# One SyncE queue in a fixed store/load order, in place of loads on SyncE and stores on GpSimd, in a decode-step backward kernel

## The chip, the cores and the metric

The kernel runs on one NeuronCore of a Trainium2 chip. The metric is the device time of one execution in microseconds (us). A time here is the median of the fast runs of one kernel. A ratio of two kernels is the mean time of one kernel's fast runs over that of the other's of the same rounds, so it is not quite the ratio of the medians quoted beside it.

Engines are named as in the profile: PE (TensorE), DVE (VectorE), ACT (ScalarE), POOL (GpSimd), SP (SyncE). Beside them the core has 16 DMA engines, which move all data. "Queue" is here a line of the page's queue part (q1 holds what SP issues, q0 what POOL issues, q10 what ACT issues), and "ring" is another word for it, where the order of the transfers waiting in it is meant.

## The reference

One decode step of attention with a key/value cache, plus a SwiGLU MLP, on a single token of width 640, forward and backward (the vector-Jacobian product), in bf16:

```python
xn = layernorm(x)
# A: 32 heads of 128, 8192 cached positions each
q = (xn @ wq)                       # wq 640 x 4096
p = softmax(q @ K^T / sqrt(128))    # K, V: 32 x 8192 x 128
attn = (p @ V) @ wo                 # wo 4096 x 640
# B: F = 1728
out = x + attn + (silu(xn @ w1) * (xn @ w3)) @ w2
# returned: out and the gradients of x, K, V, wq, wo, w1, w3, w2
```

The gradients of K and V are as large as K and V: 64 tiles of 2 MB are read and 64 written. The weights add 17 MB each way. About 303 MB cross the DMA engines in each execution.

## The kernel before

Ten SBUF slots of 2 MB hold K/V tiles. A tile is loaded, used, overwritten in place with its gradient, and stored. Its slot then takes the next load. Loads are issued on SyncE (`nc.sync`), stores on GpSimd (`nc.gpsimd`).

```python
def load_group(g):                    # weights of four heads, 2 x 640 KB
    wq_g = wpool.tile([P, NC, GW], BF16, name="wq_g", tag="wq_g")
    nc.sync.dma_start(wq_g[:], wq_v[:, :, g * GW:(g + 1) * GW])   # rows of 1024 B
    wo_g = wpool.tile([P, GH, D], BF16, name="wo_g", tag="wo_g")
    nc.sync.dma_start(wo_g[:], wo_v[:, g * GH:(g + 1) * GH, :])   # rows of 1280 B
    grp[g] = dict(wq=wq_g, wo=wo_g)

def load_next():
    if not pending:
        return
    kind, h = pending.pop(0)
    if kind == "K" and h % GH == GH - 1 and h // GH + 1 < NG:
        load_group(h // GH + 1)
    t = free_slots.pop(0)
    nc.sync.dma_start(t[:], (kc if kind == "K" else vc)[h])       # 128 rows of 16 KB
    kv_tiles[(kind, h)] = t

def store(kind, h):
    t = kv_tiles.pop((kind, h))
    nc.gpsimd.dma_start((dkc if kind == "K" else dvc)[h], t[:])
    free_slots.append(t)
    load_next()
# ... (cut: transposes, dots, softmax, outer products)
def finish_group(g):
    # ... (cut)
    nc.gpsimd.dma_start(dwo_v[:, g * GH:(g + 1) * GH, :], wo_g[:])
    # ... (cut)
    nc.gpsimd.dma_start(dwq_v[:, :, g * GW:(g + 1) * GW], wq_g[:])
# ... (cut: the MLP, which stores the gradients of w1, w2, w3 on GpSimd)
for h in range(H):
    # ... (cut)
    sums(h); outer_v(h, 0, J // 2); outer_v(h, J // 2, J)
    store("V", h)
    # ... (cut: MLP after head 1; K of head h+1; outer_k)
    store("K", h)
    # ... (cut)
```

## Time and profile before

| | before |
|---|---|
| time, us (3 runs) | 749.74 (749.73 to 751.52) |
| span of the profiled run, us | 748.2 |
| bytes moved, mean rate | 304.62 MB, 407 GB/s |

The profile's page of the kernel before: busy time of each engine, then the span in 40 equal slices (busy tenths of the DMA engines, and GB/s), then DMA queues with packets, MB and share of the 16 engines' time.

```profile
span 748.2 us, 25141 instructions
## 1 busy us (share of the span) xinstructions
PE 594.4 (79%) x11263; PEld 550.9 (74%) x11263; DVE 445.3 (60%) x771; ACT 329.8 (44%) x668; POOL 53.6 (7%) x93
...
DMA  8999999999999999999999999999998999999976
GB/s 324 387 420 423 421 422 429 427 414 430 423 420 425 424 428 422 425 429 427 390 362 411 424 428 422 379 424 430 427 417 316 423 426 430 425 427 426 425 294 259
...
q1 hardware_dynamic: 21828, 151.35, 48.9%
q0 software_dynamic: 12960, 151.34, 48.2%
q8 instruction: 88, 1.44, 0.7%
```

No compute engine is near its limit, and the DMA engines are busy almost everywhere. q1 holds the loads (SyncE), q0 the stores (GpSimd), and q8 the instruction fetches, 88 packets of 16 KB. The slices show short holes in the middle and at the end. The table of 10 us windows has them larger (columns: window and its length, busy time and count of each engine, TensorE clock, DMA share, GB/s):

```profile
core 0: us, PE busy (x) PEld busy (x) DVE busy (x) ACT busy (x) POOL busy (x), PEclk, DMA share, GB/s
380.00:390.00 10.00, 8.28 (x215) 7.92 (x214) 7.94 (x15) 3.07 (x7) 0.00 (x0) 1.00 0.80 313
560.00:570.00 10.00, 8.43 (x168) 8.08 (x169) 9.07 (x13) 5.03 (x10) 1.07 (x2) 1.00 0.73 280
720.00:730.00 10.00, 4.48 (x130) 4.29 (x131) 8.52 (x7) 0.16 (x1) 0.53 (x1) 1.00 0.46 192
```

The page's list of DMA issues (count, KB each, median us from issue to landing) shows loads waiting long behind stores, the small-row weight loads longest:

```profile
out_dram<-kv POOLq DMA_DIRECT2D x64, 2048.0 KB, 19.7
kv<-in_A_k_cache_dram SPq DMA_DIRECT2D x32, 2048.0 KB, 47.1
...
wq_g<-in_A_wq_dram SPq DMA_DIRECT2D x8, 640.0 KB, 68.0
wo_g<-in_A_wo_dram SPq DMA_DIRECT2D x8, 640.0 KB, 62.8
```

And in the list of waits PE stands still for K loads (total us, times, longest):

```profile
PE pT L260 <- DMA kv<-in_A_k_cache_dram: 70.7, 7, 24.5
```

The page's group of the K/V transposes says the same (shapes, count, busy us and mean ns; then PE's idle time before them and what ended it):

```profile
L260 PE MATMUL pT<-ident_f,kv 128*128 128x128 f32 x2048 | 334.7, 287 | 75.3 <-DMA kv<-in_A_k_cache_dram 70.7
```

### The profile page before, as it was taken

What the parts mean: (1) busy time and instruction counts of PE and PEld (TensorE: products, weight loads), DVE (VectorE), ACT (ScalarE), POOL (GpSimd) and SP (SyncE); (2) the same over time, 40 slices, a digit from 0 to 9 for tenths busy, and PEclk for the clock granted to TensorE, in tenths of its full rate; (3) what the DMA queues carried; (4) which work ended last, traced back from release to release, by engine and by line L of the source; (5) the groups of instructions that cost most, each with busy time, mean ns of one, the idle gap of its engine ahead of it and who ended that gap; (6) DMA issues with size and microseconds to landing.
All of it is one profiled execution on the core that took longest, in us unless ns stands there. A gap on an engine that the chain in (4) does not pass through costs nothing. (4 is left out here: it accounts for less than half of the span.)

```text
span 748.2 us, 25141 instructions
## 1 busy us (share of the span) xinstructions
PE 594.4 (79%) x11263; PEld 550.9 (74%) x11263; DVE 445.3 (60%) x771; ACT 329.8 (44%) x668; POOL 53.6 (7%) x93
## 2 busy tenths in 40 slices
PE   2988798993889999429986999829989499998961
PEld 2886688883778888329886888829888488887860
DVE  4368857671577657506676456653576565756664
ACT  2541254553345555215554555505555255554530
POOL 0001100100001000100001000010000100010001
PEclk9995999997799999859999899968999799999995
DMA  8999999999999999999999999999998999999976
GB/s 324 387 420 423 421 422 429 427 414 430 423 420 425 424 428 422 425 429 427 390 362 411 424 428 422 379 424 430 427 417 316 423 426 430 425 427 426 425 294 259
DMA packets 35183, 304.62 MB, mean 407 GB/s; under 512 B 2836, under 2 KB 14036, under 8 KB 18692
## 3 DMA queue, kind: packets, MB, share of 16 engines
q1 hardware_dynamic: 21828, 151.35, 48.9%
q0 software_dynamic: 12960, 151.34, 48.2%
q8 instruction: 88, 1.44, 0.7%
q10 hardware_dynamic: 288, 0.33, 0.2%
q14 instruction: 19, 0.16, 0.0%
HBM read 151.67 MB, written 151.34 MB: 405 GB/s over the span
## 5 line engine op out<-in xcount | busy, mean ns | idle before, releaser
L260 PE MATMUL pT<-ident_f,kv 128*128 128x128 f32 x2048 | 334.7, 287 | 75.3 <-DMA kv<-in_A_k_cache_dram 70.7
L262 ACT COPY KT<-pT 128x512 f32<-128x512 f32 x512 | 293.8, 588 | 227.1 <-PE pT L260 186.4
L260 PEld LDWEIGHTS pT<-ident_f,kv 128*128 128x128 f32 x2048 | 229.6, 146 | 78.3 <-issue 76.0
L271 PEld LDWEIGHTS <-KT 128*128 128x128 bf16 x4096 | 179.2, 99 | 28.4 <-ACT KT L262 19.2
L321 DVE TENSOR_TENSOR kv<-qd,U 128x4096 bf16<-128x4096 bf16 x64 | 144.3, 2285 | 48.5 <-PE hb L345 48.5
L321 DVE TENSOR_TENSOR kv<-qd,P 128x4096 bf16<-128x4096 bf16 x64 | 145.7, 2286 | 42.1 <-PE hb L340 42.1
L271 PE MATMUL sA<-cz,KT 128*128 128x64 bf16 x2048 | 100.6, 194 | 5.8 <-issue 2.4
L271 PE MATMUL dA<-cz,KT 128*128 128x64 bf16 x2048 | 98.7, 193 | 6.4 <-ACT KT L262 6.3
L345 PEld LDWEIGHTS <-kv 128*128 128x128 bf16 x2048 | 68.6, 98 | 13.2 <-issue 13.0
L345 PE MATMUL hb<-U,kv 128*128 128x64 bf16 x2048 | 69.5, 193 | 9.3 <-DVE U L342 6.4
L358 POOL DMA_DIRECT2D out_dram<-kv x64 | 34.9, 546 | 567.8 <-DVE kv L321 309.1
L340 PE MATMUL hb<-P,kv 128*128 128x64 bf16 x2048 | 69.3, 193 | 0.3 <-issue 0.3
L340 PEld LDWEIGHTS <-kv 128*128 128x128 bf16 x2048 | 68.8, 99 | 0.4 <-issue 0.4
L336 DVE SCALAR_TENSOR_TENSOR U<-dA,P 128x64 bf16<-128x64 f32 x32 | 7.4, 231 | 77.0 <-PE dA L271 77.0
L347 ACT COPY od_g<-hb 128x2 f32<-128x2 f32 x32 | 5.1, 161 | 79.0 <-PE hb L345 45.6
L285 ACT CAST qd<-pT 128x256 bf16<-128x256 f32 x32 | 12.0, 375 | 54.4 <-PE pT L282 54.4
L229 DVE SCALAR_TENSOR_TENSOR KT<-wo_g,g_bc 128x640 bf16<-128x640 bf16 x32 | 26.4, 824 | 15.9 <-PE dA L271 15.4
L308 DVE RECIPROCAL rZ<-sA 128x1 f32<-128x1 f32 x32 | 5.4, 169 | 47.1 <-PE sA L301 47.1
L293 DVE TENSOR_REDUCE mrow<-sA 128x1 f32<-128x64 f32 x32 | 6.5, 203 | 33.3 <-PE sA L271 33.2
L384 DVE SCALAR_TENSOR_TENSOR wq_g<-wq_g,KT 128x512 bf16<-128x512 bf16 x40 | 26.2, 686 | 0.0
L297 DVE TENSOR_REDUCE negM<-sA 128x1 f32<-128x128 f32 x32 | 9.3, 291 | 14.5 <-PE sA L294 14.5
L301 PEld LDWEIGHTS sA<-rsum,pm_one 128*128 128x128 f32 x64 | 9.5, 187 | 11.2 <-ACT E L300 11.2
(127 smaller groups left out, 311.2 us busy)
## 6 DMA issues: line engine op xcount, KB each, us to landing
out_dram<-kv POOLq DMA_DIRECT2D x64, 2048.0 KB, 19.7
kv<-in_A_k_cache_dram SPq DMA_DIRECT2D x32, 2048.0 KB, 47.1
kv<-in_A_v_cache_dram SPq DMA_DIRECT2D x32, 2048.0 KB, 40.9
wq_g<-in_A_wq_dram SPq DMA_DIRECT2D x8, 640.0 KB, 68.0
wo_g<-in_A_wo_dram SPq DMA_DIRECT2D x8, 640.0 KB, 62.8
out_dram<-wo_g POOLq DMA_DIRECT2D x8, 640.0 KB, 16.1
out_dram<-wq_g POOLq DMA_DIRECT2D x8, 640.0 KB, 18.4
kv<-in_B_w_dram SPq DMA_DIRECT2D x2, 1728.0 KB, 18.5
```

The source lines that it names most:

```text
L229: nc.vector.scalar_tensor_tensor(junk, wo_g[:, hh, :], 1.0, g_bc[:], ALU.mult, ALU.mult, accum_out=do_c[:, hh:hh + 1])
L260: nc.tensor.transpose(pT[:, k * P:(k + 1) * P], W3[:, 4 * c + k, :], ident_f[:])
L262: nc.scalar.copy(KT[:].rearrange("p k w -> p (k w)"), pT[:])
L271: nc.tensor.matmul(out_[:, 0:J], lhsT=KTb[:, k, par, :], rhs=cz[:, par, a, J - 2 - 2 * i:ZW - 2 * i], start=(i == 0 and par == 0), stop=(p ...
L285: nc.scalar.copy(qd[:].rearrange("p a d -> p (a d)"), ps_r[:, 0:2 * DH])
L297: nc.vector.tensor_reduce(negM[:], sA[:, J:J + P], AX.X, ALU.max, negate=True)
L301: nc.tensor.matmul(sA[:, J + P:J + P + 1], lhsT=ones_b, rhs=rsum[:], start=False, stop=True, skip_group_check=True)
L321: nc.vector.tensor_tensor(dst[:, lo * DH:hi * DH].rearrange("p (j a b) -> p j a b", a=DH // 2, b=2), vec.rearrange("p (a b) -> p a b", b=2 ...
L340: nc.tensor.matmul(hb[:, 0:RW], lhsT=V3[:, j, :], rhs=P2[:, j, 0:1].to_broadcast([P, RW]), start=False, stop=(j == J - 1), skip_group_chec ...
L345: nc.tensor.matmul(hb[:, RW:2 * RW], lhsT=K3[:, j, :], rhs=U2[:, j, 0:1].to_broadcast([P, RW]), start=False, stop=(j == J - 1), skip_group ...
L358: nc.gpsimd.dma_start((dkc if kind == "K" else dvc)[h], t[:])
L384: nc.vector.scalar_tensor_tensor(wq_g[:, ci, :], wq_g[:, ci, :], 1.0, dqb, ALU.mult, ALU.mult, accum_out=dxa[:, ci, g:g + 1])
```

## The change

Intent: with one queue in program order, a weight load no longer competes with the stores' larger packets, and loads and stores take turns, one 2 MB tile each. `lag` keeps one more slot back, so that a load goes into the slot whose store was issued one store earlier, and the wait for that store leaves transfers behind it in the ring. The two small final outputs move to ScalarE's queue.

```diff
+    def fifo(out_, in_):
+        tc.keep_in_program_order(nc.sync.dma_start(out_, in_))
 ...
+    lag = [1]                      # set to 2 after the first loads
     def load_next():
-        if not pending:
+        if not pending or len(free_slots) < lag[0]:
             return
 ...
-        nc.sync.dma_start(t[:], (kc if kind == "K" else vc)[h])
+        fifo(t[:], (kc if kind == "K" else vc)[h])
 ...
     def store(kind, h):
-        nc.gpsimd.dma_start((dkc if kind == "K" else dvc)[h], t[:])
+        fifo((dkc if kind == "K" else dvc)[h], t[:])
 ...                               # likewise every weight load (nc.sync -> fifo)
 ...                               # and every weight-gradient store (nc.gpsimd -> fifo)
-    nc.sync.dma_start(out_0 ..., fin_bf[0:NC, :])
+    nc.scalar.dma_start(out_0 ..., fin_bf[0:NC, :])        # out_1 likewise
```

More of the change, by code (lines that the diff above doesn't have):

```diff
@@ L101, in load_group @@
         wq_g = wpool.tile([P, NC, GW], BF16, name="wq_g", tag="wq_g")
-        nc.sync.dma_start(wq_g[:], wq_v[:, :, g * GW:(g + 1) * GW])
+        fifo(wq_g[:], wq_v[:, :, g * GW:(g + 1) * GW])
         wo_g = wpool.tile([P, GH, D], BF16, name="wo_g", tag="wo_g")
-        nc.sync.dma_start(wo_g[:], wo_v[:, g * GH:(g + 1) * GH, :])
+        fifo(wo_g[:], wo_v[:, g * GH:(g + 1) * GH, :])
         grp[g] = dict(wq=wq_g, wo=wo_g)
@@ L138 @@
         nc.vector.memset(w2b[RB:P, NFULL - NBA, :], 0.0)
-        nc.sync.dma_start(w2b[0:RB, NFULL - NBA, :], B_w2[NFULL * P:F, :])
-    nc.sync.dma_start(w2a, B_w2[0:NBA * P, :].rearrange("(fb p) c -> p fb c", p=P))
-    nc.sync.dma_start(w2b[:, 0:NFULL - NBA, :],
+        fifo(w2b[0:RB, NFULL - NBA, :], B_w2[NFULL * P:F, :])
+    fifo(w2a, B_w2[0:NBA * P, :].rearrange("(fb p) c -> p fb c", p=P))
+    fifo(w2b[:, 0:NFULL - NBA, :],
                       B_w2[NBA * P:NFULL * P, :].rearrange("(fb p) c -> p fb c", p=P))
-    nc.sync.dma_start(w1a, w1_v[:, 0:NA, :])
-    nc.sync.dma_start(w1b, w1_v[:, NA, :])
-    nc.sync.dma_start(w3a, w3_v[:, 0:NA, :])
-    nc.sync.dma_start(w3b, w3_v[:, NA, :])
+    fifo(w1a, w1_v[:, 0:NA, :])
+    fifo(w1b, w1_v[:, NA, :])
+    fifo(w3a, w3_v[:, 0:NA, :])
+    fifo(w3b, w3_v[:, NA, :])
     for _ in range(2):
         load_next()
+    lag[0] = 2
     ident_f = consts.tile([P, P], F32, name="ident_f")
@@ L381, in finish_group @@
             nc.vector.tensor_scalar(wo_g[:, hh, :], g_bc[:], od[:, hh, 0:1], None, ALU.mult)
-        nc.gpsimd.dma_start(dwo_v[:, g * GH:(g + 1) * GH, :], wo_g[:])
+        fifo(dwo_v[:, g * GH:(g + 1) * GH, :], wo_g[:])
         for ci in range(NC):
@@ L386, in finish_group @@
             nc.vector.tensor_scalar(wq_g[:, ci, :], dqb, xn_col[:, ci:ci + 1], None, ALU.mult)
-        nc.gpsimd.dma_start(dwq_v[:, :, g * GW:(g + 1) * GW], wq_g[:])
+        fifo(dwq_v[:, :, g * GW:(g + 1) * GW], wq_g[:])
     def wrow(wi, ci):
@@ L456, in mlp @@
             nc.vector.tensor_scalar(w2a[:, b, :], g_bc[:], hcol[:, b:b + 1], None, ALU.mult)
-        nc.gpsimd.dma_start(out_8[0:NBA * P, :].rearrange("(fb p) c -> p fb c", p=P), w2a)
+        fifo(out_8[0:NBA * P, :].rearrange("(fb p) c -> p fb c", p=P), w2a)
         for b in range(NBA, NB):
             nc.vector.tensor_scalar(w2b[:, b - NBA, :], g_bc[:], hcol[:, b:b + 1], None, ALU.mult)
-        nc.gpsimd.dma_start(out_8[NBA * P:NFULL * P, :].rearrange("(fb p) c -> p fb c", p=P),
+        fifo(out_8[NBA * P:NFULL * P, :].rearrange("(fb p) c -> p fb c", p=P),
                             w2b[:, 0:NFULL - NBA, :])
         if RB:
-            nc.gpsimd.dma_start(out_8[NFULL * P:F, :], w2b[0:RB, NFULL - NBA, :])
+            fifo(out_8[NFULL * P:F, :], w2b[0:RB, NFULL - NBA, :])
         free_slots.append(mD)
@@ L490, in mlp @@
                 nc.vector.tensor_scalar(wa[:, ci, :], bc_sb[:, wi, :], xn_col[:, ci:ci + 1], None, ALU.mult)
-            nc.gpsimd.dma_start(dv[:, 0:NA, :], wa)
+            fifo(dv[:, 0:NA, :], wa)
             free_slots.append((mA, mB)[wi])
@@ L501, in mlp @@
             nc.vector.tensor_scalar(wb, bc_sb[:, wi, :], xn_col[:, NA:NC], None, ALU.mult)
-            nc.gpsimd.dma_start(dv[:, NA, :], wb)
+            fifo(dv[:, NA, :], wb)
         free_slots.append(mC)
@@ L557 @@
     nc.vector.tensor_copy(fin_bf[:], ps_o[0:2 * NC, 0:P])
-    nc.sync.dma_start(out_0.rearrange("a b (c p) -> (a b c) p", p=P), fin_bf[0:NC, :])
-    nc.sync.dma_start(out_1.rearrange("a b (c p) -> (a b c) p", p=P), fin_bf[NC:2 * NC, :])
+    nc.scalar.dma_start(out_0.rearrange("a b (c p) -> (a b c) p", p=P), fin_bf[0:NC, :])
+    nc.scalar.dma_start(out_1.rearrange("a b (c p) -> (a b c) p", p=P), fin_bf[NC:2 * NC, :])
 _INS = ['A_x', 'A_k_cache', 'A_v_cache', 'A_wq', 'A_wo', 'B_x', 'B_w1', 'B_w3', 'B_w2', 'grad_out']
```

## The prediction

> **What bounds the kernel now.** The DMA engines. The page's queue part shows 304.62 MB in a span of 748.2 us, the load and store queues holding 48.9% and 48.2% of it; the slices show 420 to 430 GB/s in most places. PE is 79% busy, DVE 60%, ACT 44%.
>
> The visible losses are small: in a table of 10 us windows 370-400 moves 366, 313 and 387 GB/s, 470-490 387 and 374, 560-580 280 and 353, 720-730 192. Against 425 GB/s these are 15 to 18 us of the mean engine. That looks like the prize, 2%.
>
> But the trace's packet records say more. From the first transfer to the last there is no instant without a data packet in flight, 743.9 us. In the deepest holes one of 16 engines is still working (7.1 us in total), and at the end one finishes 4 us after the others. Of each load's 16 completions the last comes up to 20 us after the fifteenth. One engine is always behind, hence always busy. It seems to be the one that also fetches instructions: 88 packets of 16 KB, spread evenly. Around one such fetch the interval between kv packets grew from 611 to 725 ns; I estimate 0.25 us a fetch, 22 us in all. A mean engine works about 724 us; 724 + 22 is about the 744 seen. So the straggler is the bound, and the holes are the others waiting for it.
>
> **What the change removes, adds, moves.** It removes the software queue and the competition between rings. Now 1 KB weight packets alternate with 16 KB store packets: weight loads land after 63 to 68 us (median), kv stores after 20; PE starves up to 25 us for a K load. The Trainium skill, "DMA: Bandwidth & Descriptors", section "Queues, rings and completion order", describes this round robin by packet; the trace agrees. These waits should go. By the same page, section "Issuing engines are not separate DMA queues", both queues use the same 16 engines, so no bandwidth is added; here a 16 KB packet takes 611 ns in either queue.
>
> Added: weight-gradient stores probably split like weight loads: 1024 B in 46 ns, 1280 B in 55, 3456 B in 138, instead of 4096 B in 160, 5120 in 198, 6912 in 262. Estimate over 12,224 pieces: 4.5 us per engine. A load waits for the store two places ahead, so two transfers (10 us) stay queued: no hole. The last 10 kv stores follow all loads, 50 us of queued work that hides the last compute.
>
> **On the critical path.** Only the straggler's own work: 744, plus up to 4.5, minus a few us of two-ring overhead. Holes filled on the other 15 engines buy nothing.
>
> **Prediction: 748 us, 8 in 10 between 738 and 757.** Faster by over 2%: 0.10; within 2%: 0.84; slower: 0.06.
>
> **What would show it.** Right: one hardware queue, half loads and half stores; no long K-load waits that leave the DMA idle; weight loads landing sooner; holes gone, mean rate still 403 to 412 GB/s; the last of 16 completions still late. Wrong: 425 GB/s throughout and a span near 725 us, meaning the straggler was no bound.
>
> **What would make it wrong.** Slower small HBM writes from the hardware queue (12,224 pieces at 30 ns more are 23 us); SyncE held by a DVE wait in the MLP stage with loads behind it; or a straggler cost that comes from the software queue and vanishes (about 730).

## More of the kernel before

`sums(h)`, used in some experiments, is two loops of 64 matmuls, each with its own weight load.

All runs here were taken in several sessions, on more than one chip; the kernel before took 749.8 to 750.5 us (medians) in each, so a difference of under 1 us between runs of different sessions says little.

## The result

The changed kernel takes 758.75 us (758.61 to 759.70, 4 runs), the kernel before 750.01 us in the same rounds: ratio 1.0115, 95% interval 1.0098 to 1.0133. It is slower by 1.15%, inside the 2% band that the prediction favoured, but 1.75 us above the range.

The same parts of the page, of the changed kernel:

```profile
span 756.8 us, 25031 instructions
## 1 busy us (share of the span) xinstructions
PE 601.0 (79%) x11263; PEld 561.1 (74%) x11263; DVE 447.1 (59%) x771; ACT 330.7 (44%) x668; POOL 0.7 (0%) x6
...
DMA  8999999999999999999999999999999999999996
GB/s 332 389 420 413 401 418 410 416 427 403 426 424 388 416 396 428 421 426 381 403 427 368 400 404 401 429 420 413 359 429 409 360 416 383 427 425 420 391 418 263
...
q1 hardware_dynamic: 43616, 302.69, 98.3%
q8 instruction: 88, 1.44, 0.7%
```

One queue now carries everything. The deep holes are gone, but many slices are at 359 to 405 GB/s although the DMA share is at 9 tenths: the engines are busy and move less.

Its DMA issues:

```profile
out_dram<-kv SPq DMA_DIRECT2D x64, 2048.0 KB, 21.2
kv<-in_A_k_cache_dram SPq DMA_DIRECT2D x32, 2048.0 KB, 15.7
...
wq_g<-in_A_wq_dram SPq DMA_DIRECT2D x8, 640.0 KB, 21.0
wo_g<-in_A_wo_dram SPq DMA_DIRECT2D x8, 640.0 KB, 22.6
```

The weight loads land after 21 to 23 us instead of 63 to 68, and in the page's groups PE's idle time before the K/V transposes fell from 75.3 us to 0.1:

```profile
L267 PE MATMUL pT<-ident_f,kv 128*128 128x128 f32 x2048 | 317.5, 287 | 0.1
```

The change did what it was meant to do. It bought no time.

Where the rate falls is seen with SyncE's instructions in order of time around one set of weight loads of the changed kernel (start, length, what), and beside it the table of 2 us windows:

```profile
578.27 0.43 SPq L99 DMA_DIRECT2D wq_g<-in_A_wq_dram  x1
578.74 0.61 SPq L99 DMA_DIRECT2D wo_g<-in_A_wo_dram  x1
587.77 6.95 SPq L99 DMA_DIRECT2D kv<-in_A_k_cache_dram  x1
594.77 0.49 SPq L99 DMA_DIRECT2D out_dram<-kv  x1
...
614.04 0.73 SPq L99 DMA_DIRECT2D out_dram<-wq_g  x1
614.87 10.16 SPq L99 DMA_DIRECT2D out_dram<-kv  x1
```

```profile
core 0: us, PE busy (x) PEld busy (x) DVE busy (x) ACT busy (x) POOL busy (x), PEclk, DMA share, GB/s
586.00:588.00 2.00, 2.00 (x38) 1.97 (x35) 0.00 (x0) 1.75 (x3) 0.00 (x0) 1.00 1.01 426
...
594.00:596.00 2.00, 2.00 (x59) 2.00 (x56) 2.00 (x2) 0.16 (x1) 0.00 (x0) 1.00 0.92 234
596.00:598.00 2.00, 2.00 (x32) 1.90 (x30) 2.00 (x2) 1.75 (x4) 0.00 (x0) 1.00 0.74 313
598.00:600.00 2.00, 2.00 (x37) 1.96 (x36) 2.00 (x1) 1.64 (x4) 0.00 (x0) 1.00 1.09 400
600.00:602.00 2.00, 1.43 (x31) 1.18 (x28) 0.46 (x3) 1.10 (x2) 0.00 (x0) 1.00 0.97 257
```

(A packet counts wholly in the window in which it starts, so a share can be above 1.) Of the 16 issues of a K/V transfer right behind weight transfers, 11 take over 2 us, most of them 7 to 10; the median of the other K/V issues is 0.43. About the end of the weight transfers the rate falls to 234 and 313 GB/s (there some engines are idle, share 0.74) and some microseconds later once more to 257, at a share of 0.97.

The trace also records every DMA packet with its start, length and size. Summed and divided by 16, they give what one engine spends on average:

| one mean engine, us | before | after |
|---|---|---|
| 16,384 packets of 16 KB, time beyond 611 ns each (the median) | 9.5 | 22.7 |
| all smaller data packets | 92.7 | 96.6 |
| idle: share of 16 that is not in flight, first to last packet | 18.2 | 12.4 |
| first to last packet, wall time | 743.9 | 753.6 |

(The rows do not add up to the last one: packets overlap, and more than 16 are in flight for 108 us before and for 122 us after. Instruction fetches count as in flight.) The smaller packets grew by 4.0 us, near the predicted 4.5. What was not predicted is the first row (below it is called the excess, in the expectations also the stretch): a 16 KB packet takes 633 ns on average instead of 620, and packets of over 760 ns went from 250 to 657. They stand in clusters among and after weight transfers: 509 of the 657 start less than 10 us after the start of a weight packet, of all 16 KB packets 41% do.

### The profile page after: what moved, and what is told of

Same layout as the page of the kernel before. It is cut to its first block, busy times and chain, and to the rows that moved or that the text cites. A ratio compares the mean times of both kernels' runs of the same rounds, so it can differ in the third digit from the quotient of the medians.

```text
span 756.8 us, 25031 instructions
## 1 busy us (share of the span) xinstructions
PE 601.0 (79%) x11263; PEld 561.1 (74%) x11263; DVE 447.1 (59%) x771; ACT 330.7 (44%) x668; POOL 0.7 (0%) x6
## 5 line engine op out<-in xcount | busy, mean ns | idle before, releaser
L269 ACT COPY KT<-pT 128x512 f32<-128x512 f32 x512 | 289.9, 588 | 120.7 <-PE pT L267 74.1
L267 PE MATMUL pT<-ident_f,kv 128*128 128x128 f32 x2048 | 317.5, 287 | 0.1
L278 PEld LDWEIGHTS <-KT 128*128 128x128 bf16 x4096 | 176.6, 99 | 30.8 <-ACT KT L269 21.5
L352 PE MATMUL hb<-U,kv 128*128 128x64 bf16 x2048 | 74.8, 199 | 42.1 <-DVE U L349 41.0
L352 PEld LDWEIGHTS <-kv 128*128 128x128 bf16 x2048 | 73.4, 102 | 45.3 <-issue 45.1
L347 PE MATMUL hb<-P,kv 128*128 128x64 bf16 x2048 | 67.7, 192 | 0.0
L347 PEld LDWEIGHTS <-kv 128*128 128x128 bf16 x2048 | 67.3, 98 | 0.0
L308 PE MATMUL sA<-rsum,pm_one 128*128 128x1 f32 x64 | 12.2, 260 | 22.6 <-ACT E L307 22.1
L307 ACT ACTIVATE E<-sA,negM 128x64 f32<-128x64 f32 x32 | 10.1, 314 | 44.2 <-DVE negM L304 44.1
```

The source lines that it names most:

```text
L267: nc.tensor.transpose(pT[:, k * P:(k + 1) * P], W3[:, 4 * c + k, :], ident_f[:])
L269: nc.scalar.copy(KT[:].rearrange("p k w -> p (k w)"), pT[:])
L278: nc.tensor.matmul(out_[:, 0:J], lhsT=KTb[:, k, par, :], rhs=cz[:, par, a, J - 2 - 2 * i:ZW - 2 * i], start=(i == 0 and par == 0), stop=(p ...
L307: nc.scalar.activation(E[:], sA[:, 0:J], ACTF.Exp, bias=negM[:], scale=1.0, accum_out=rsum[:])
L308: nc.tensor.matmul(sA[:, J + P:J + P + 1], lhsT=ones_b, rhs=rsum[:], start=False, stop=True, skip_group_check=True)
L347: nc.tensor.matmul(hb[:, 0:RW], lhsT=V3[:, j, :], rhs=P2[:, j, 0:1].to_broadcast([P, RW]), start=False, stop=(j == J - 1), skip_group_chec ...
```

## The experiments

Two theories were set against each other first. Theory 1: the weight transfers, now in the same ring as all else, cost the time. Theory 2: K/V loads and stores taking turns in one ring, or SyncE's gate, cost it. A third theory, S, is the prediction's: one DMA engine, the one that fetches instructions, bounds both kernels. Kernels called "transfers alone" have all compute taken out: the same tiles are loaded and stored back, and results are wrong.

### a_wstores_pool: weight-gradient stores back on GpSimd

```diff
-        fifo(dwo_v[...], wo_g[:])                 # and dwq, dw1, dw2, dw3
+        nc.gpsimd.dma_start(dwo_v[...], wo_g[:])
```

> The changed kernel, but the weight-gradient stores go back to the GpSimd queue; K/V loads, K/V stores and weight loads stay in the one SyncE order. Theory 1 (the weight transfers in the hardware queue cost the time: smaller packets, and the engines run dry behind them and restart with slow 16 KB packets): about half of the loss goes, 749 to 754 us, the small-packet sum falls by about 4.5 us an engine, and the clusters of slow 16 KB packets behind the weight stores go while those behind the weight loads stay. Theory 2 (loads and stores of K/V alternating in one ring are slow in themselves, or SyncE's gating is): 757 to 759 us, stretch of 16 KB packets near 22 us as in the changed kernel.

Measured: 753.72 us (752.69 to 755.74), ratio to before 1.0048 (1.0032 to 1.0065). The result is correct. 5.0 us of the loss went. The small packets fell from 96.6 to 92.9 us an engine and the excess of the 16 KB packets from 22.7 to 17.0 us. That is as theory 1 said.

### b_allw_pool: weight loads on GpSimd as well

```diff
-        fifo(wq_g[:], wq_v[...])                  # and wo, w1, w2, w3
+        nc.gpsimd.dma_start(wq_g[:], wq_v[...])
```

> The changed kernel, but all weight loads and all weight-gradient stores go to the GpSimd queue; the K/V loads and stores alone keep the one SyncE order. Theory 1 (weight transfers in the hardware queue): the stretch of the 16 KB packets falls from 22.7 us to under 10 us an engine, holes of SyncE go, 740 to 748 us, at or below the kernel before. Theory 2 (alternating K/V in one ring): stays at 753 us or more, and the stretch stays near 20 us.

Measured: 751.26 us (750.73 to 752.57), ratio 1.0015 (1.0000 to 1.0030). The result is correct. 7.5 us of the loss are gone, and what is left against the 750.2 of the kernel before is 1 us. So weight transfers in the one ring make nearly all of the change's loss. But the time lies between the ranges of the two theories and is not "at or below the kernel before", and the excess of the 16 KB packets was 21.6 us, not under 10. So in the whole kernel that sum does not follow the time. Cleaner runs were needed.

### d_after_fewer_pe and e_before_fewer_pe: fewer PE instructions

In both kernels the two loops of 64 matmuls in `sums` were cut to one matmul each (wrong result).

```diff
-        for j in range(J):
+        for j in range(J - 1, J):
```

> The changed kernel with the 64 matmuls of each of the two hb sums of a head cut to one (wrong result on purpose; all DMA bytes the same). About 4000 matmuls with their weight loads less, so instruction fetches should fall from 88 to about 57. Theory S (one DMA engine also fetches the instructions and is the last by that): the lag of the last of 16 completions at the end falls from 4.5 us to about 3, and the time falls by 31 fetches of about 0.15 to 0.25 us, 4 to 8 us, to 751 to 755 us. Rival (the straggler has nothing to do with instruction fetch, all engines bound the kernel alike): within 2 us of 758.8.

Measured: 747.07 us (743.63 to 751.83), 11.7 us less than the changed kernel and 4 us below the range of theory S. Fetches fell from 88 to 57. In the last transfer the last of the 16 completions came 3.3 us after the fifteenth, before it was 4.5.

> The kernel before with the same cut of about 4000 matmuls (wrong result on purpose; all DMA bytes the same). Theory S (the engine that fetches instructions is the bound of the kernel before too): 31 fetches less at the 0.38 us each that the changed kernel gave, 737 to 743 us, and the last engine's lag at the end under 3 us. Rival (in the kernel before the holes in the slices are the loss, the straggler only follows): 746 us or more, with the holes still there.

Measured: 743.61 us (738.69 to 744.28), ratio 0.9890 (0.9865 to 0.9915), with 56 fetches. The median is 0.6 us above the range. The lag at the end did not shrink: 8.0 us against 3.6 us in the kernel before, a miss. Both times fall as theory S says, but by 0.38 us for each fetch that went in d and by 0.20 in e, and the cut also shortened compute, so they do not prove it. Their times also spread more than those of other kernels.

### f_dma_only_after and g_dma_only_before: transfers alone

```diff
     for h in range(H):
-        ...                                       # all compute
         store("V", h)                             # MLP stores after head 1
         store("K", h)                             # weight stores after every fourth head
```

> The changed kernel's DMA order alone, no compute (wrong result on purpose): every load and store in the same SyncE order, stores wait only for their loads. Theory 1 and 2 both say the slow packets come from the pattern of transfers: then the clusters of slow 16 KB packets stay (stretch 15 to 23 us) and the time falls only by what instruction fetch and waits for compute cost, to 740 to 748 us. Rival (the slow packets and holes come from SyncE held by compute, that is by the DVE waits): stretch under 5 us, time 726 to 735 us.

Measured: 734.77 us (733.96 to 735.91), excess of the 16 KB packets 13.2 us. The time is at the edge of the rival's range; the excess fits neither (under 5, or 15 to 23) and is nearer the theories' range. Much of the slow packets stays without compute, so it belongs to the transfers, and far more than foreseen of the rest of the time (24 us) belongs to what compute brings with it.

> The transfers of the kernel before alone, no compute (wrong result on purpose): loads in the SyncE queue, stores in the GpSimd queue. The changed order alone took 734.8 us. Theory P (one ring that alternates tile by tile brings the slow 16 KB packets, whatever the compute does): here the stretch stays under 6 us and the time is 4.5 us (store pieces) plus 7 to 11 us lower, 720 to 728 us. Rival (the pattern of transfers is no worse than two rings; the changed kernel lost by how its order meets the compute): 729 to 735 us, only the 4.5 us of the pieces apart.

Measured: 718.05 us (717.91 to 718.30), excess 0.5 us. The single ring in the fixed order costs 16.7 us, with no compute and no instruction fetch in either run. That is more than either theory said (the time lies below both ranges). The DMA part of the page, first of f_dma_only_after, then of g_dma_only_before:

```profile
GB/s 324 392 430 414 419 417 410 421 431 422 419 430 383 424 395 430 429 423 421 399 432 425 390 419 414 430 419 434 387 431 432 380 423 405 432 429 429 418 430 316
...
q1 hardware_dynamic: 43616, 302.69, 99.9%
```

```profile
GB/s 319 428 420 411 430 426 426 428 434 428 425 429 431 430 430 425 429 432 431 418 431 433 429 430 426 426 433 431 430 423 430 431 432 426 426 430 432 432 431 333
...
q1 hardware_dynamic: 21808, 151.34, 50.3%
q0 software_dynamic: 12960, 151.34, 49.6%
```

The dips to 380 to 405 GB/s, once every few slices, are a matter of the order of transfers alone. Two rings have none of them.

### h_lag3: one more transfer behind the gate

```diff
-    lag[0] = 2
+    lag[0] = 3
```

> The changed kernel with each load one place later (a load waits for the store three places ahead, so three transfers stay queued at that moment in place of two). Theory Q (the ring runs short behind the gate, the engines run dry and restart in step): holes and clusters of slow packets shrink, stretch under 15 us, 748 to 754 us. Rival (queue depth plays no part): 757 to 760 us, stretch 20 to 24 us.

Measured: 761.53 us (760.99 to 762.68), excess 21.8 us. The result is correct. A deeper ring did not help, it was 2.8 us slower (and so above the rival's range too). The theory that more transfers behind the gate shorten the loss fell. SyncE's issues of K/V right behind weights were now held for 16.0 us (median of 16) in place of 7.0.

### j_dma_only_two_hw: two rings, both hardware

Transfers alone, in the order of the kernel before, with the stores in ScalarE's queue.

```diff
-        nc.gpsimd.dma_start(...)                  # every store
+        nc.scalar.dma_start(...)
```

> Transfers alone again, loads in the SyncE queue and stores in ScalarE's queue: two rings, both hardware (wrong result on purpose). Theory P (single ring alternating): stretch under 6 us, 4 to 5 us (the store pieces) above the run with GpSimd stores, about 725 to 732 us. Rival (the hardware queue's stores are slow in themselves): 733 us or more, stretch over 10 us, as with all in one ring.

Measured: 718.66 us (718.40 to 719.03), excess 0.4 us, below both ranges. So the hardware queue stores as fast as the software queue. The smaller pieces of its weight stores, which the prediction costed at 4.5 us, cost 0.6 us against the run with GpSimd stores (718.05). This run and f_dma_only_after move the same pieces, all by hardware queues, in two rings and in one. Of the 16.1 us between them (17.1 in span), the packet records place 12.8 us an engine in slower 16 KB packets, 2.9 in idle time and 1.2 in the small packets.

### k, l, m: which property of the single ring

All three are transfers alone. k takes the weights out of the ring. l keeps one ring, but does two stores, then two loads. m keeps the changed kernel's order and gate, and issues the stores on ScalarE.

```diff
 k:  -  fifo(wq_g[:], ...)  ... fifo(dwq_v[...], ...)     # every weight load and store
 k:  +  nc.gpsimd.dma_start(...)
 l:     free_slots.append(t)
 l:  -  load_next()
 l:  +  if kind == "K":
 l:  +      load_next()
 l:  +      load_next()
 m:  -  fifo((dkc if kind == "K" else dvc)[h], t[:])      # every store
 m:  +  tc.keep_in_program_order(nc.scalar.dma_start(...))
```

> Transfers alone (wrong result on purpose): K/V loads and stores in the one SyncE order, weight loads and weight-gradient stores in the GpSimd queue. One ring for everything took 734.8 us, two rings 718.0 and 718.7. Theory W (the small-piece weight transfers inside the single ring are the cost: the ring runs dry behind them and the 16 KB packets after them are slow): 717 to 722 us, stretch under 4 us. Rival D (K/V loads and stores taking turns in one ring is the cost): 729 to 735 us, stretch 9 us or more.

> Transfers alone, all in one SyncE ring, but two K/V stores, then two K/V loads, in place of one and one (wrong result on purpose); half as many changes of direction. Rival D (a change of direction in the ring costs): half of the 16 us goes, 724 to 730 us. Theory W (weight transfers in the ring): unchanged, 732 to 737 us.

> Transfers alone, loads in the SyncE queue in the changed kernel's order and with its gate (a load goes into the slot of the store two places ahead), stores in ScalarE's queue in program order (wrong result on purpose). If the single ring is the cost, 717 to 722 us and stretch under 2 us, as with the other two-ring runs; if the gate or the fixed order is, 728 us or more.

| transfers alone | us (4 runs each) | excess of 16 KB packets, us |
|---|---|---|
| g: two rings, GpSimd stores | 718.05 | 0.5 |
| j: two rings, ScalarE stores | 718.66 | 0.4 |
| m: two rings, changed order and gate | 718.56 | 0.3 |
| k: one ring for K/V, weights on GpSimd | 721.74 | 5.7 |
| l: one ring, pairs | 733.79 | 10.4 |
| f: one ring, the changed kernel's order | 734.77 | 13.2 |

m shows that in two rings neither the fixed order nor the gate costs anything. l shows that halving the changes of direction is worth at most about 1 us (l and f are from different sessions). k shows that 13.0 of the 16.7 us go when the weight transfers leave the ring; its excess of 5.7 is above the 4 that was expected, and the 3.7 us that it keeps over g are not explained.

So the cost comes from weight transfers in a ring that carries everything else too. Sharing a ring is not enough: in g, j and m the weight loads go with the K/V loads and the weight stores with the K/V stores, and nothing is lost. Nor is a held SyncE enough. In g, too, its issues behind weight loads are held, and for longer (start, length, what):

```profile
456.11 19.25 SPq L104 DMA_DIRECT2D wo_g<-in_A_wo_dram  x1
475.46 32.94 SPq L118 DMA_DIRECT2D kv<-in_A_k_cache_dram  x1
```

Between 450 and 510 us of this run the DMA engines still move 424 to 435 GB/s (10 us windows), for GpSimd goes on issuing stores. That in one ring the hold costs because SyncE can issue no stores either would fit k, where no issue of SyncE takes over 1 us. It was not tested.

The page of k_dma_only_w_pool has no dips in its second half, where f_dma_only_after has four at 380 to 405 (the last slice is the end of the program in both):

```profile
GB/s 336 397 420 428 409 422 397 420 428 417 429 422 423 419 428 419 422 428 431 429 430 431 430 431 432 429 433 431 431 431 430 432 431 430 432 431 431 432 430 310
```

### n_before_row_sums: an attempt at a faster kernel

If fetches bound the kernel, fewer PE instructions should make it faster. The sums were recast as 16 matmuls of 512 columns with 4-column weights, and 4 short ones that pick the four diagonal blocks, on top of the kernel before.

```diff
-        for j in range(J):
-            nc.tensor.matmul(hb[:, 0:RW], lhsT=V3[:, j, :], rhs=P2[:, j, 0:1].to_broadcast([P, RW]), ...)
+        for c in range(J // 4):
+            nc.tensor.matmul(hb[0:4, :], lhsT=w[:, 4 * c:4 * c + 4, 0],
+                             rhs=X[:, 4 * c * DH:4 * (c + 1) * DH], start=(c == 0), stop=(c == J // 4 - 1))
+        ...                                       # copy, then 4 matmuls [4 x 128] x [4 x 1]
```

> The kernel before with the two hb sums of a head done as 16 matmuls with 512 columns and 4 short ones each, in place of 64 (right result); about 6000 PE instructions pairs fewer, so some 45 fetches fewer of 88 at most, DMA traffic of the data unchanged. Theory S (the engine that fetches instructions is the bound): 738 to 744 us, faster than both kernels. Rival: within 2 us of 750.

Measured: 833.15 us (830.80 to 836.98), ratio 1.1102. The result is correct. It failed for another reason than the one it was to test, and only 20 fetches went, not 45. The page of n_before_row_sums:

```profile
PE 763.1 (92%) x8703; PEld 555.6 (67%) x8703; DVE 444.5 (53%) x739; ACT 357.1 (43%) x732; POOL 53.4 (6%) x93
...
q8 instruction: 68, 1.11, 0.5%
```

PE is now busy for 92%, 763 us, which is more than the whole kernel before took, so it is taken to be the bound. In the timeline 16 of the wide matmuls take 3.62 us, where 64 of the old ones took 2.12. No version that beats the kernel before came out.

### o, p, q: instruction fetches without compute

These three test theory S without its mixture with compute. Transfers alone, and beside them PE runs matmuls on constant tiles that wait for no transfer and that no transfer waits for.

```diff
+    for _ in range(11000):                        # q: 3100, with 512 columns
+        nc.tensor.matmul(dp[:, 0:128], lhsT=dw[:], rhs=dx[:], start=True, stop=True)
```

> The transfers of the kernel before alone (718.0 us), and beside them 11,000 pairs of weight load and matmul (128 columns) on constant tiles, which wait for no transfer and which no transfer waits for (wrong result on purpose). Instruction fetches should come back to about 86. Theory S (the fetches slow one DMA engine): 740 to 752 us, the last engine finishing 3 us or more after the others. Rival (what the whole kernel adds over its transfers are waits for compute): 717 to 722 us.

> The changed kernel's transfers alone (734.8 us), with the same 11,000 independent pairs on PE. If fetches explain both kernels, this gives 755 to 760 us, that is about 24 us more, and the gap of 16.7 us between the two orders shrinks to about 9, as between the two whole kernels. If the gap stays at 14 us or more, the shrinking comes from compute and not from the fetches.

> As the two-ring run with independent PE work, but 3,100 pairs with 512 columns: PE about as busy with a fifth to a third of the instructions, about 24 fetches. Theory S: 722 to 728 us, in proportion to the fetches. Rival (a busy PE itself slows the transfers): within 5 us of the run with 11,000 pairs.

| | transfers alone, us | with PE work, us | fetches | added, each fetch |
|---|---|---|---|---|
| o, two rings | 718.05 | 743.96 | 86 | 25.9, 0.30 |
| q, two rings | 718.05 | 724.32 | 24 | 6.3, 0.26 |
| p, one ring | 734.77 | 754.55 | 86 | 19.8, 0.23 |

Lines of the pages of o_two_rings_many_pe and then of q_two_rings_few_pe:

```profile
PE 616.4 (83%) x11000; PEld 616.3 (83%) x11000; DVE 0.7 (0%) x4; POOL 52.6 (7%) x91
...
q8 instruction: 86, 1.41, 0.7%
```

```profile
PE 667.5 (92%) x3038; PEld 303.7 (42%) x3100; DVE 1.0 (0%) x4; POOL 52.6 (7%) x91
...
q8 instruction: 24, 0.39, 0.2%
```

In q PE is busier than in o, and the transfers lose a quarter as much: the loss goes with the fetches, not with a busy PE. (Fetches and PE instructions change together, 86 for 22,000 and 24 for 6,200, so the runs alone cannot tell one from the other.) In the last transfer of o the last completion comes 8.4 us after the fifteenth, of q 2.0 us, of g, with no fetch, 0.2 us. So one engine is late, and the more so the more fetches there are. That it is late because all fetches run on it is inferred from this; the records do not name engines.

p is 0.45 us under its range. Between the two orders the gap is 16.7 us without fetches, 10.6 us with them (o to p), and 8.7 us in the whole kernels.

## Why the prediction was right or wrong

- **What bounds the kernel: right, as far as the runs can tell.** Transfers alone take 718 us. 86 fetches put 25.9 us on top (o), and the whole kernel adds 32. A fetch was estimated at 0.25 us, and each added 0.23 to 0.30. There is luck in that: the one interval that the prediction quotes, 611 ns grown to 725, gives 0.11 us. So filling the holes that show on the other engines bought nothing, as predicted. The chance of over 2% faster (0.10) was rightly small, and the class, within 2%, was right. This was in part luck: the 16.7 us that the prediction missed are 2.2% of 750, and only because the straggler hid a part did the kernel stay within 2%.
- **What it removes: right.** Weight loads land after 21 to 23 us instead of 63 to 68, PE no longer stands for K loads, the last compute is hidden.
- **"Two transfers stay queued: no hole": half right.** The holes from starved loads went, but about the end of weight transfers there are new ones (234 to 313 GB/s in the 2 us windows shown). The mean rate came out at 402 GB/s, just under the 403 to 412 given.
- **The small pieces, 4.5 us: the records agree, the cost does not.** The records' sum grew by 4.0 us, but two rings with the same pieces lost only 0.6 us. Adding packet lengths overstated it.
- **The step that failed** is the last term of the sum, "minus a few us of two-ring overhead", with its ground, "a 16 KB packet takes 611 ns in either queue". 611 ns is the median in every run, but not the mean: 624 ns with everything in one ring and nothing else running (f), 611 in two (g, j, m). In its place the runs showed, with nothing else running, that going to one ring costs plus 16.7 us instead of minus a few. Of these 13.0 leave with the weight transfers, and in the whole kernel 7.5 of about 8.5 us do. The straggler hides a part: fetches cost 6.1 us less in the slower ring (19.8 against 25.9), which leaves 10.6. The whole kernel lost 8.7; the last 1.9 us are not assigned.
- **Named fears.** "Slower small HBM writes from the hardware queue" were not the cause: j stored the same pieces from a hardware queue in 718.66 us. "SyncE held by a DVE wait" was not the cause either: f has no compute and shows the loss.
- **Open.** Why the 16 KB packets that follow weight transfers in the same ring are slow is not settled. SyncE's issue of the next tile is held 7 to 10 us there, but in g it is held for longer and nothing is lost, and more transfers behind the gate did not help (h). What would tell is one ring for everything and a second ring with some other steady traffic. The excess of 21.6 us in b_allw_pool, which lost little time, is not explained, nor are the 3.7 us of k. Of what the whole kernels add over transfers with fetches (6 us before, 4 after), no run says what it is.

The Trainium skill, "DMA: Bandwidth & Descriptors", section "Issuing engines are not separate DMA queues", says that transfers issued from different engines run on the same 16 DMA engines and interleave, and that issuing on several saves only the sequencer's time. The runs agree on bandwidth (no slice of a page here is above 434 GB/s, with one ring or two). On the rest they differ in size at least: the page calls that time usually small, and here one ring took 734.8 us and two took 718.0. Whether the loss goes through SyncE's time is open. The skill's "Perfetto Trace Analysis", section "DMA Optimizations", says that one issuing engine for inputs and another for outputs may make sense, above all with loops or control flow. Here that arrangement was the faster one (718.0 against 734.8 us) in straight-line code too.

## What to carry to other kernels

Before filling holes in a DMA-bound profile, see whether all 16 engines have them: compare the last of a transfer's 16 completions with the one before, and count the instruction fetches, because this kernel, with 22,500 PE instructions and weight loads, seems to be bound by the engine that fetches them. If one ring carries everything, take the transfers of small rows out of it, or give loads and stores a ring each: here either was worth 13 us or more of 735. To cost an order of transfers, run the transfers alone: here that took one short kernel and gave the difference that packet lengths had missed.

## What the Trainium skill lacked or had wrong

- "Runtime: NRT & Kernel Launch", section "Instruction fetch mechanics", says that instructions are refilled in blocks of 16 KiB over a DMA queue of their own (the trace agrees: 88 packets of 16 KB) and calls the cost of crossing a block boundary "mostly hidden". It seems not to be hidden in a DMA-bound program: PE work with 86 fetches added 25.9 us to 718.05, with 24 it added 6.3. No page looked up says that one DMA engine is late where there are fetches (8.4 us at the end with 86 fetches, 0.2 with none).
- "DMA: Bandwidth & Descriptors", section "Issuing engines are not separate DMA queues", lacks that one ring can be slower than two on the same engines: 734.8 against 718.0 and 718.7 us, with 1 to 3.5 KB weight packets between 16 KB ones.
- The same page lacks that the issue of a transfer behind one of many small rows can hold the issuing engine: 6.95 and 10.16 us in the changed kernel, where the median of the other K/V issues is 0.43, and 32.94 in g.
